# Layer 2's transform over d by frequency modulo four, a third X buffer, copies on another queue, and new orders in a two-layer spectral and mixer kernel

## The chip, the cores and the metric

The kernel runs on one core of a Trainium2 chip. Its time is the device time of one execution in microseconds (us), the median over runs. A core has a matrix engine, TensorE (PE in the profile, its weight loads PEld), a vector engine (DVE), a scalar engine (ACT), GpSimd (POOL), and SyncE (SP), whose queue here holds only DMA issues. Each engine works through its own instructions in the order in which the program wrote them; a semaphore holds an instruction until what it needs is there, and everything behind it on that engine waits with it.

## The reference

x has 2048 rows of 512 numbers. Two layers of the same form follow each other, each of two parts:

```python
x = x + _A_ref(_layernorm(x, axis=-1), A_w_r, A_w_i)
x = x + _B_ref(_layernorm(x, axis=-1), B_w1, B_w2, B_w3, B_w4)
```

`_A_ref` is a spectral filter: a real two-dimensional Fourier transform over rows and columns, a product with the complex table W = w_r + i w_i, and the transform back. `_B_ref` is a mixer: a layer norm, a product with w1 (512 x 512), a gelu, four column groups shifted by -1, +1, -2 and +2 rows, a product with w2 and a residual; then a layer norm, w3 (512 x 1792), a gelu, w4 (1792 x 512) and a residual.

## The kernel before, in words

Row s of x is row p of tile q with s = 16 p + q, so `K.x` holds 16 tiles q of 128 x 512. A layer's spectral part runs in these stages, and the letters are those of the order strings:

- front: per tile q the statistics of its rows (`s`, aggregated by `i`), the root (`S`), its reciprocal (`J`), the table T scaled by it (`Q`), then the transform over p as matmuls with x as the stationary operand (`O`), and copies out of PSUM into V (`G`). `over_p_quarters` issues eight matmuls a tile (four of 256 columns, four of 128), `over_p` four of 256, `over_p_plain` four of 128 whose sums and differences DVE forms while it copies (`fold_V`).
- d: the transform over d (`over_d`), copied to TV (`t`); q: the transform over q with the tables TL, in matmuls of 64 rows, two at a time (`over_q`), copied to X (`x`); p: the product with W on DVE (`weigh`), into PB; b: back over q with TR (`back_q`), copied to M (`m`). The unit is a block b of two frequencies over p, or a pair of blocks.
- D: back over d with G (`back_d`), copied to Y (`Y`); P: back over p (`back_p`), added to x by DVE (`a`).

The mixer follows: squares on ACT (`s`), statistics on POOL (`r`), root and reciprocal (`e`, `i`), the normed rows (`n`), transposed by DMA (`T`), w1 and its gelu (`v`, `h`), w2 (`u`), residuals (`f`, `E`), norm, transpose, w3 and gelu (`R`, `o`, `U`, `w`, `g`), w4 and the residual (`W`, `A`). The next layer's front is woven into the w3 and w4 work, and in the last layer the stores (`y`).

Three strings hold the order of all this, written out by hand or by a planner: `ORDER_0` for the first front, `ORDER_A` and `ORDER_B` for the two layers. An entry is a letter, a number (tile, block or pair) and, after it, the engine (A, V, P) or the PSUM bank (.0 to .7). `X` issues matmuls on zeros that only keep PE busy. In `first_front` the statistics of tiles 5 and 9 are made on ACT (`ON_ACT`), by two passes of ACT and, on POOL, `from_means` (L376 to L378, entry `f`). Entry `f2` also calls `load_tables` (L196, L188, L189), the POOL-issued loads of FL, TL and TR; `f3` stands behind it on POOL.

Layer 1's d works by the frequency modulo four (tables FL). Layer 2's d works with FA, by the frequency modulo two; W's columns are therefore permuted in place by DVE during layer 1's mixer (`permute`, entries `L`, L813 and L814), and G is loaded again in permuted order (`load_G2`). W comes in 16 loads on SyncE's queue; every second partition is a copy of its neighbour, made by four DMAs within SBUF (`double`), issued by POOL. All G, Tinv and MLP weights stand on SyncE's queue behind a small load that waits for the last of these copies.

## Time and profile before

| what | us |
|---|---|
| median of three runs | 347.29 (347.23 to 347.61) |
| profiled execution, first to last instruction (the span) | 345.6 |
| PE / DVE / ACT / POOL busy | 336.6 / 187.5 / 195.5 / 62.8 |
| w3 and w4 matmuls (L735, L755), together, on the chain | 56% of the span |
| first front matmul | 8.19 |
| last W load landed | 22.7 |

A table of stretches, used below, gives for a stretch of the span the busy time of each engine with its number of instructions, the granted clock of PE as a share, the DMA share and the rate in GB/s. A timeline line gives the start, the time from the first start to the last end, the engine and source line, the operation, out and in, and how many were merged; what ended idle time before them stands in brackets. A line of groups gives the busy time and mean ns of one, then the idle time ahead of it. An instruction's duration includes its latency, so the next one of the same kind starts before it ends.

The profile was taken in an execution of its own[...].

### The profile page before, as it was taken

The numbers are of one execution on the slowest core, as the hardware profiler recorded it, in microseconds if no ns is written. First come the engines' busy times: TensorE is split into PE (matmuls) and PEld (weight loads), VectorE is DVE, ScalarE is ACT, GpSimd is POOL, SyncE is SP. The second block draws the span as 40 slices with busy tenths as digits, with TensorE's granted clock in tenths as the row PEclk, the third lists the DMA queues.
The fourth block names the chain that finished last, engine by engine and source line by source line (L and its number), as shares of the span: only waits on it lengthen the run. The fifth ranks groups of instructions, "written<-read, shape, count | busy, mean of one in ns | idle before, by whom it ended". The sixth has DMA issues, their size and how long they took to land.

```text
span 345.6 us, 5672 instructions
## 1 busy us (share of the span) xinstructions
PE 336.6 (97%) x2161; PEld 190.3 (55%) x2178; DVE 187.5 (54%) x448; ACT 195.5 (57%) x348; POOL 62.8 (18%) x157
## 2 busy tenths in 40 slices
...
GB/s 259 280 361 236 383 173 101 84 62 0 3 61 21 33 24 14 49 13 1 2 0 2 2 2 44 99 97 41 27 2 61 0 108 0 46 14 95 0 32 76
DMA packets 45834, 25.12 MB, mean 73 GB/s; under 512 B 35008, under 2 KB 42816, under 8 KB 45808
## 3 DMA queue, kind: packets, MB, share of 16 engines
...
q10 hardware_dynamic: 240, 0.10, 0.1%
...
## 4 chain that ended last, share of the span: by engine, by line
PE 83%; ACT 7%; DVE 5%; DMA 3%; issue 2%; SPq 0%; ACTq 0%; DVEq 0%
PE ps L735 28%; PE ps L755 28%; PE ps L700 8%; PE ps L684 7%; PE ps L431 3%; PE ps L632 2%; PE ps L614 2%; ACT xn L306 2%; PE ps L644 1%; ACT hT L159 1%; DVE PB L603 1%; PE ps L584 1%; ACT X L159 1%; DVE X L157 1%; DVE x_state L652 1%
## 5 line engine op out<-in xcount | busy, mean ns | idle before, releaser
L742 ACT ACTIVATE gT<-ps 128x1024 bf16<-128x1024 f32 x56 | 56.6, 1023 | 80.4 <-PE ps L735 79.7
L735 PE MATMUL ps<-xT,w 128*128 128x512 bf16 x448 | 99.3, 379 | 0.0
L755 PE MATMUL ps<-w,gT 128*128 128x512 bf16 (+1 forms) x464 | 98.3, 366 | 0.6
L755 PEld LDWEIGHTS <-gT 128*128 128x128 bf16 x476 | 46.5, 98 | 50.1
L735 PEld LDWEIGHTS <-w 128*128 128x128 bf16 x448 | 43.8, 98 | 52.6
L761 DVE TENSOR_TENSOR x_state<-ps,x_state 128x512 bf16<-128x512 f32 (+1 forms) x34 | 22.1, 657 | 86.1 <-PE ps L755 78.9
L708 DVE SCALAR_TENSOR_TENSOR xn<-xn,ln_c,ps 128x512 bf16<-128x512 bf16 x32 | 23.5, 745 | 26.3 <-PE ps L700 19.5
L700 PE MATMUL ps<-w,hT 128*128 128x512 bf16 x123 | 28.8, 379 | 0.3
L684 PE MATMUL ps<-xT,w 128*128 128x512 bf16 x128 | 28.8, 379 | 0.2 <-DMA xT<-xn 0.2
L306 ACT ACTIVATE junk<-xn 128x512 bf16<-128x512 bf16 x32 | 19.9, 622 | 12.7 <-DVE xn L708 12.7
L652 DVE SCALAR_TENSOR_TENSOR x_state<-ps,x_state 128x512 bf16<-128x512 f32 x32 | 20.5, 686 | 4.2 <-PE ps L644 4.1
L294 DVE BATCH_NORM_STATS2 ln_st<-x_state 128x6 f32<-128x512 bf16 (+1 forms) x31 | 20.1, 663 | 3.7 <-DMA x_state<-in_A_x_dram 3.5
L700 PEld LDWEIGHTS <-hT 128*128 128x128 bf16 x128 | 12.4, 98 | 15.3 <-ACT hT L691 0.8
L684 PEld LDWEIGHTS <-w 128*128 128x128 bf16 x128 | 12.3, 98 | 15.3 <-DMA xT<-xn 1.4
L312 POOL TENSOR_SCALAR ln_mv<-ln_s 128x4 f32<-128x4 f32 x16 | 5.7, 357 | 80.3 <-DVE x_state L652 68.7
L306 ACT ACTIVATE xn<-x_state 128x512 bf16<-128x512 bf16 x32 | 20.0, 631 | 0.4 <-DVE x_state L652 0.2
L603 DVE TENSOR_TENSOR PB<-X,W 128x2048 bf16<-128x2048 bf16 (+1 forms) x20 | 19.4, 1010 | 0.2
L691 ACT ACTIVATE hT<-ps 128x512 bf16<-128x512 f32 x32 | 17.4, 604 | 2.5 <-PE ps L684 2.4
L314 POOL TENSOR_TENSOR ln_mv<-ln_s,ln_t 128x4 f32<-128x4 f32 x16 | 3.8, 239 | 80.1 <-ACT junk L306 73.5
L614 PE MATMUL ps<-TR,PB 128*128 128x128 bf16 x256 | 16.3, 219 | 0.1
L159 ACT ACTIVATE TV<-ps 128x1024 bf16<-128x1024 f32 (+1 forms) x16 | 14.2, 914 | 3.8 <-PE ps L560 2.3
L644 PE MATMUL ps<-Y,Tinv 128*128 128x256 bf16 x128 | 15.4, 272 | 0.5 <-ACT Y L159 0.2
...
## 6 DMA issues: line engine op xcount, KB each, us to landing
w<-in_B_w_dram SPq DMA_DIRECT2D x2, 1792.0 KB, 13.0
...
```

The lines of the kernel that those rows point to most:

```text
L159: K.nc.scalar.activation(dst, src, ACT.Copy, bias=0.0, scale=1.0)
L306: K.nc.scalar.activation(out, src, ACT.Square, bias=0.0, scale=D ** -0.5, accum_out=self.s[:, i, 1:2])
L603: nc.vector.tensor_tensor(t, X.pop(u)[:, 0:2 * n].unsqueeze(1).to_broadcast([P, 2, 2 * n, 256]), K.W[:, :, 2 * u:2 * u + 2 * n, 1:257], op ...
L614: nc.tensor.matmul(oh, lhsT=pab[u][:, k, 2 * (b - u) + h, F * P:(F + 1) * P], rhs=K.TR[:, k:k + 2, 2 * b + h], start=(k == 0), stop=(k == 1))
L652: nc.vector.scalar_tensor_tensor(K.x[:, q, :], ps.pop(("P", q)), 1.0, K.x[:, q, :], op0=ALU.mult, op1=ALU.add, accum_out=ln[g].s[:, i, 0:1])
L684: nc.tensor.matmul(o[:, i], lhsT=K.w1[:, t, j * P:(j + 1) * P], rhs=xT[g][:, :, t, :], start=(t == 0), stop=(t == 3))
L700: nc.tensor.matmul(o, lhsT=K.hT[:, j, st:st + P], rhs=K.w2[:, j, :], start=(j == 0), stop=(j == 3))
L708: nc.vector.scalar_tensor_tensor(xn[:, q, :], xn[:, q, :], ln[q // 4].c[:, q % 4:q % 4 + 1], ps.pop(("u", n)), op0=ALU.mult, op1=ALU.add, ...
L735: nc.tensor.matmul(o[:, i], lhsT=K.w3[:, c, t * P:(t + 1) * P], rhs=xT3[g][:, :, c, :], start=(c == 0), stop=(c == 3))
L742: nc.scalar.activation(gT[g][:, 2 * j:2 * j + 2, :], ps.pop(("w", k)), ACT.Gelu_apprx_tanh, bias=0.0, scale=1.0)
L755: nc.tensor.matmul(o, lhsT=gT[g][:, t, i * P:(i + 1) * P], rhs=K.w4[:, t, d], start=(t == 0), stop=(t == 13))
L761: nc.vector.tensor_tensor(x, ps.pop(("W", n)), x, op=ALU.add)
```

## The change

- Layer 2's d uses the same code and tables as layer 1's; FA, G2 and both permutations go. V is then needed in four quarters: `fold_V` makes two of them and the sums, `fold_again` (entry `I`, on DVE or POOL) the other two.
- Layer 2's front has six plain pairs where it had five; the others use `over_p_quarters`. That function interleaves the two tiles of a pair in PSUM, in runs of four columns, and the copies can be split in halves by block (`SPLIT_FIRST`, `SPLIT_V`, entries `L`).
- The four last blocks of back q are made and copied in halves (`SPLIT_B`, entries `V` and `l`), and back d is issued in two halves (`D` and `C`).
- X has three buffers, T's scaled tables eight where they had twelve.
- W's copies 1 to 3 are issued on SyncE's queue behind the W loads; copy 0 stays on POOL.
- POOL can take rows of a layer norm (`apply`), residuals (`resid`) and folds; ACT can make scaled tables in layer 2's front.
- All three orders are new. `FOLD`, `half_D` and `fold_D`, also new, are used by no entry.

Of `ORDER_A` and `ORDER_B` the diff below has the part up to the first w1 product. Of the code, some hunks are left out.

```diff
-    double = lambda k: q.dma_start(K.W[1::2, :, 8 * k:8 * k + 8], K.W[0::2, :, 8 * k:8 * k + 8])
+    double = lambda k, q=nc.gpsimd: q.dma_start(K.W[1::2, :, 8 * k:8 * k + 8], K.W[0::2, :, 8 * k:8 * k + 8])
 
     def load_tables():
-        spare = K.grp.tile([P, 4, 4, P], BF16, name="xT", bufs=4)
-        K.FL = spare[:, 0:2].rearrange("p a b c -> p (a b c)")[:, 0:768]
-        K.dummy = spare[:, 2, 0:1]
-        q.dma_start(K.FL, dram["FL"])
+        K.FL = K.const.tile([P, 768], BF16, name="FL")
+        q.dma_start(K.FL[:], dram["FL"])
         load_TL(0)
         load_TL(1)
         load_TR(0)
@@ -203,19 +196,12 @@
         gate = K.const.tile([1, 2], BF16, name="gate")
         q.tensor_copy(gate[:], after[0:1, 0, 0:2])
         turn_TL(K, slice(0, 8))
-        double(1)
         q.dma_start(K.TL[:, 1, 8:16], dram["TL2"])
-        double(2)
-        double(3)
         load_TR(1)
+        for k in range(1, 4):
+            double(k, nc.sync)
 
...
             setattr(K, k, t)
-        K.FA = K.const.tile(list(tabs["FA"].shape), BF16, name="FA")
-        for t in range(2):
-            nc.sync.dma_start(K.FA[:, t], dram["FA"][:, t])
 
...
-        if eng == "V":
-            self.K.nc.vector.tensor_scalar(dst, src, self.mv[:, i, 0:1], r, op0=ALU.add, op1=ALU.mult)
+        if eng in "VP":
+            e = self.K.nc.vector if eng == "V" else self.K.nc.gpsimd
+            e.tensor_scalar(dst, src, self.mv[:, i, 0:1], r, op0=ALU.add, op1=ALU.mult)
...
-    K.Tq[q] = K.stream.tile([P, 2, P], BF16, name="Tq", bufs=12)
+    K.Tq[q] = K.stream.tile([P, 2, P], BF16, name="Tq", bufs=8)
...
-def over_p(K, qs, split=False):
-
...
+def over_p_quarters(K, qs):
+
+    n = len(qs)
+    ps = banks(K, n)
     for i, q in enumerate(qs):
         T = K.Tq.pop(q)
-        plus, both, swap = T[:, 0], T[:], T[:, ::-1]
-        twice = lambda k: T[:, k:k + 1].to_broadcast([P, 2, P])
+        plus, both, swap = [v.rearrange("d k (b c) -> d k b c", c=4) for v in (T[:], T[:], T[:, ::-1])]
+        plus = plus[:, 0]
+        twice = lambda k: T[:, k:k + 1].to_broadcast([P, 2, P]).rearrange("d k (b c) -> d k b c", c=4)
         for h in range(2):
-            o = (ps[:, h, 0:256] if split else ps[:, i, h * 256:(h + 1) * 256]).rearrange("d (k p) -> d k p", k=2)
+            o = (ps[:, h] if n == 2 else ps[:, 0, h * 256:(h + 1) * 256]).rearrange("d (k b q c) -> d k b q c", k=2, q=n, c=4)
+            o = o[:, :, :, i]
             terms = ((0, o, twice(0)), (1, o[:, 1], plus), (3, o[:, 1], plus), (2, o, swap)) if h == 0 else \
                     ((1, o, swap), (0, o[:, 0], plus), (2, o[:, 0], plus), (3, o, twice(1)))
-            for n, (c, dst, rhs) in enumerate(terms):
-                K.nc.tensor.matmul(dst, lhsT=K.x[:, q, c * P:(c + 1) * P], rhs=rhs, start=(n == 0), stop=(n == 3))
...
-def fold_V(K, qs, ps, right):
+def fold_V(K, qs, ps, right, pairs):
+
     n, lo = len(qs), qs[0]
-    v = K.V[:].rearrange("d (t h) b q c -> d h t q b c", h=2)[:, :, :, lo:lo + n]
-    left = ps[:, :, 0:256].rearrange("d q (t b c) -> d t q b c", t=2, c=4)
-    right = right.rearrange("d q (t b c) -> d t q b c", t=2, c=4)
-    for h, op in ((0, ALU.add), (1, ALU.subtract)):
-        for t in range(2):
-            K.nc.vector.tensor_tensor(v[:, h, t], left[:, t], right[:, t], op=op)
-
-
-def take_V(K, qs, ps, eng, part=False):
+    row = lambda t: t.rearrange("d q (t b c) -> d t q b c", t=2, c=4)
+    v = K.V[:].rearrange("d t b q c -> d t q b c")[:, :, lo:lo + n]
+    for t in range(2):
+        K.nc.vector.tensor_tensor(v[:, 3 * t], row(ps[:, :, 0:256])[:, t], row(right)[:, t], op=ALU.subtract)
+    K.nc.vector.tensor_tensor(pairs, ps[:, :, 0:256], right, op=ALU.add)
...
+def fold_again(K, qs, pairs, eng):
+
+    n, lo = len(qs), qs[0]
+    e = K.nc.vector if eng == "V" else K.nc.gpsimd
+    row = pairs.rearrange("d q (t b c) -> d t q b c", t=2, c=4)
+    v = K.V[:].rearrange("d t b q c -> d t q b c")[:, :, lo:lo + n]
+    for t, op in ((1, ALU.add), (2, ALU.subtract)):
+        e.tensor_tensor(v[:, t], row[:, 0], row[:, 1], op=op)
...
+def take_V(K, qs, ps, eng, half=None):
 
     dst = K.V[:].rearrange("d t b q c -> d (t b) q c")[:, :, qs[0]:qs[-1] + 1:max(qs[-1] - qs[0], 1)]
-    if part:
-        t = "AV".index(eng)
-        dst, ps = dst[:, 64 * t:64 * t + 64], ps[:, t:t + 1, 0:256]
-    copy(K, dst, ps.rearrange("d q (tb c) -> d tb q c", c=4), eng)
+    src = ps.rearrange("d n (s q c) -> d (n s) q c", q=len(qs), c=4)
+    if half is not None:
+        lo = slice(16 * half, 16 * half + 16)
+        dst, src = [v.rearrange("d (t b) q c -> d t b (q c)", t=4)[:, :, lo] for v in (dst, src)]
+    copy(K, dst, src, eng)
...
-            if not last:
-                oi = o[:, i].rearrange("p (e r f) -> p e r f", e=2, r=4)
-                part = lambda k: V[:, k, 2 * b:2 * b + 2].rearrange("d b q c -> d (b q c)")
-                nc.tensor.matmul(oi[:, :, 3], lhsT=part(1), rhs=K.FL[:, 0:P].rearrange("p (e f) -> p e f", e=2),
-                                 start=True, stop=True)
-                nc.tensor.matmul(oi[:, :, 1], lhsT=part(2), rhs=K.FL[:, P:2 * P].rearrange("p (e f) -> p e f", e=2),
-                                 start=True, stop=True)
-                for k in range(2):
-                    rhs = K.FL[:, (k + 1) * 256:(k + 2) * 256].rearrange("p (e r f) -> p e r f", e=2, r=2)
-                    nc.tensor.matmul(oi[:, :, 0:3:2], lhsT=part(3 * k), rhs=rhs, start=(k == 0), stop=(k == 1))
-                continue
-            oi = o[:, i].rearrange("p (e h f) -> p h e f", e=2, h=2)
-            for h in range(2):
-                for t in range(2):
-                    nc.tensor.matmul(oi[:, 1 - h], rhs=K.FA[:, t, h],
-                                     lhsT=V[:, 2 * t + h, 2 * b:2 * b + 2].rearrange("d b q c -> d (b q c)"),
-                                     start=(t == 0), stop=(t == 1))
+            oi = o[:, i].rearrange("p (e r f) -> p e r f", e=2, r=4)
+            part = lambda k: V[:, k, 2 * b:2 * b + 2].rearrange("d b q c -> d (b q c)")
+            nc.tensor.matmul(oi[:, :, 3], lhsT=part(1), rhs=K.FL[:, 0:P].rearrange("p (e f) -> p e f", e=2),
+                             start=True, stop=True)
+            nc.tensor.matmul(oi[:, :, 1], lhsT=part(2), rhs=K.FL[:, P:2 * P].rearrange("p (e f) -> p e f", e=2),
+                             start=True, stop=True)
+            for k in range(2):
+                rhs = K.FL[:, (k + 1) * 256:(k + 2) * 256].rearrange("p (e r f) -> p e r f", e=2, r=2)
+                nc.tensor.matmul(oi[:, :, 0:3:2], lhsT=part(3 * k), rhs=rhs, start=(k == 0), stop=(k == 1))
...
-        X[u] = K.stream.tile([P, 4, 256], BF16, name="X", bufs=2)
+        X[u] = K.stream.tile([P, 4, 256], BF16, name="X", bufs=3)
...
-        both = TAKE_B[last][b] == "B"
-        ps["b", b] = o = banks(K, 1 + both)
-        for F in range(2):
+        ps["b", b, F] = o = banks(K, 1)[:, 0]
+        parts = (0, 1) if F is None else (F,)
+        for i, f in enumerate(parts):
             for h in range(2):
...
-    def back_d(m):
-        ps["D", m] = o = banks(K, 2)
-        for F in range(2):
-            for i in range(2):
-                for e in range(2):
-                    nc.tensor.matmul(o[:, i, e * 256:(e + 1) * 256], lhsT=M[:, F, e, 2 * m + i, :], rhs=K.G[:, F, e, :],
-                                     start=(F == 0 and e == 0), stop=(F == 1 and e == 1))
+        n = 512
+        if F is not None:
+            dst, n = dst[:, :, 2 * F:2 * F + 2], 256
+        copy(K, dst, ps.pop(("b", b, F))[:, 0:n].rearrange("f (h g q c) -> f h g q c", h=2, q=NQ, c=4), eng)
+
+    def first_half(b):
+        return 0 if b in SPLIT_B[last] else None
+
+    def back_d(m, F):
+        if F == 0:
+            ps["D", m] = banks(K, 2)
+        o = ps["D", m]
+        for i in range(2):
+            for e in range(2):
+                nc.tensor.matmul(o[:, i, e * 256:(e + 1) * 256], lhsT=M[:, F, e, 2 * m + i, :], rhs=K.G[:, F, e, :],
+                                 start=(F == 0 and e == 0), stop=(F == 1 and e == 1))
...
-    def resid(n):
-        nc.vector.tensor_tensor(K.x[:, ROWS[n], :], K.x[:, ROWS[n], :], xn[:, ROWS[n], :], op=ALU.add)
+    def resid(n, eng):
+        (nc.vector if eng == "V" else nc.gpsimd).tensor_tensor(K.x[:, ROWS[n], :], K.x[:, ROWS[n], :], xn[:, ROWS[n], :], op=ALU.add)
...
     def front(k):
         qs = [ROWS[n] for n in PAIRS[k]]
-        ps["O", k] = over_p_plain(K, qs) if k < PLAIN else over_p(K, qs, k >= 14)
-
-    def take_front(k, eng):
+        ps["O", k] = over_p_plain(K, qs) if k < PLAIN else over_p_quarters(K, qs)
+
+    def take_front(k, eng, half=0):
...
-                fold_V(K, qs, ps["O", k], ps["right", k][:])
+                ps["pairs", k] = K.stream.tile([P, 2, 256], FP32, name="pairs", tag="TV_Y", bufs=4)
+                fold_V(K, qs, ps["O", k], ps["right", k][:], ps["pairs", k][:])
...
-    def permute(k):
-
-        w = K.W[:, k // 8, 4 * (k % 8):4 * (k % 8) + 4, 1:257]
-        t = K.stream.tile([P, 4, 256], BF16, name="X", bufs=2)
-        tw = t[:]
-        nc.vector.tensor_copy(tw.rearrange("p b (h f) -> p b h f", h=2), w.rearrange("p b (f h) -> p b h f", h=2))
-        nc.vector.tensor_copy(w, tw)
...
-TAKE_B = ("FFFFFFFFFFFFFFFB", "FFFFFFFFFFFFFFFB")
+SPLIT_B = ((12, 13, 14, 15), (12, 13, 14, 15))
+SPLIT_FIRST = (5, 6, 7, 8)
+SPLIT_V = (6, 14, 15)
 ROWS = [*range(2, 16), 0, 1]
 PAIRS = {**{k: [2 * k, 2 * k + 1] for k in range(7)}, 14: [14], 15: [15]}
-PLAIN = 5
-FLEX = "mGnotxY"
+PLAIN = 6
+FLEX = "mlGLnotxYIKEpQ"
+FOLD = [(), ()]
...
 ORDER_0 = """
-s0 s1 s3 i1 i0 s2 s4 i3 i2 S0 J0 Q0V s5 i4 S1 J1 Q1A O0 s6 s7 i6 i7 s8 Q2A Q3A O1 f2 S2 J2 i8 Q6V Q7V s9 f3 s10 O3 Q4V
-Q5A s11 O2 G0A i10 i11 s13 S3 G1A J3 Q8V Q10A Q11A Q9V O4 s12 i13 i12 S4 G3A s15 s14 J4 i15 i14 Q12V S5 Q13V G2A G4A
-J5 Q14V O5 Q15V O6 G5V O7 G7A G6V O8 G8A G8V
+s0 s1 i0 i1 s2 s3 S0 J0 s5 i2 i3 Q1V Q0V O0.0 S1 J1 f2 s9 s8 s10 s11 i8 i10 f3 i11 s7 Q2A Q3A O1.2 S3 J3 Q11A i7 Q9A
+Q10A Q8V s6 s4 i6 i4 G1A s13 S2 J2 s12 Q4A O4.4 G4A Q6V Q5V i13 i12 s14 S4 Q7A J4 O5.6 s15 i14 i15 G0A Q12V Q13V S5
+G5A J5 O2.2 O3.4 L5A G3A Q14V Q15V G2V O6.0 L6V G6A O8.6 O7.7 G8A L8A L7A G7V
 """
...
 ORDER_A = """
-d0.3 t0V d1.6 d2.0 t1A q0.2 x0V p0 t2A q1.4 x1A p1 d4.6 t4A N0 d10.1 t10A q2.4 x2V p2 q4.6 d6.0 x4A t6A d12.3 t12A
-d14.5 q10.6 q6.0 d8.2 p4 x10A b4.4 x6V b3.7 d15.6 p10 t8A m4A t15A p6 q8.2 q12.0 b1.4 m3A x8A b0.6 b2.7 x12A b6.2 m2A
-t14V b5.3 m1V p8 q15.0 m0A q14.4 b10.7 x15A b9.6 p12 m6A m10V p15 b8.0 m5A x14A b7.2 m7A b11.3 m11A p14 b12.7 m8V
-b13.5 m9V b14.1 m12A b15.2 m13A m14A X4.0 m15A m15V D1.5 Y1A D0.0 Y0A D3.3 Y3A P2.5 a2 s2 P3.6 a3 s3 P0.0 a0 P7.2 s0
-P1.7 P6.5 D2.0 a1 s1 a7 s7 r0 a6 s6 Y2V e0 i0 n1V D5.6 Y5A n0V T0 D4.2 Y4A P4.0 a4 P5.4 a5 s4 n3V D7.5 s5 r1 Y7A n2V
-P8.7 P11.3 c0 a8 a11 e1 i1 n4V n5V T1 P10.4 D6.0 Y6A s8 a10 s10 P15.5 T2 P14.3 n7V n6V s11 P9.2 P12.0 c1 a9 s9 P13.4
...
+X4.0 d0.3 t0A d2.0 d1.5 q0.2 d4.6 t1A N0 t2V x0A p0V t4A q1.4 x1A q2.0 x2V d6.2 t6A d10.6 q4.4 p1V t10A d14.0 x4V t14A
+d8.2 q10.6 q6.4 t8A x10A p2V d15.0 x6A p4V b2.1 q14.2 x14A m2V d12.6 p10V q8.1 b1.5 t15A b3.0 t12A p6V x8A b10.4 q15.6
+m10A b0.3 x15A q12.1 p14V b4.4 b14.6 p8V m0A b11.7 m3V p15V b5.3 x12A b8.0 m11A b6.1 b15.2 p12V b7.7 m8V m4A b13.4 m1A
+m15A m5A m13V m6A b12.5 m12V m14A V15.2 b9.0 m9A V13.3 l13A V14.5 V12.4 m7V D0.6 D1.0 l14A l15V l12V C1 Y1A C0 D3.2 C3
+Y3A P2.0 P3.1 Y0V P1.7 D2.2 P0.6 a2 s2 C2 D5.4 C5 a3 s3 a1 s1 P7.7 D7.0 a0 s0 r0 Y2V Y5A a7 P5.6 P6.2 e0 i0 n1P n0P s7
+a5 s5 P4.3 a6 s6 a4 n3V s4 P11.4 D4.6 C4 C7 P10.5 D6.2 C6 T0 n2P Y7A T1 r1 Y4V P9.6 P8.7 e1 Y6A P15.0 P12.1 P13.2 a11
+i1 n6V s11 n7V T3 a9 s9 a10 s10 a8 s8 n5P P14.3 n4P v0.4 h0 r2 T2 v1.6 h1 a15 M1 a14 n11V n10V v3.4 T5 s15 n8P v2.6 M0
...
 """
 ORDER_B = """
-d15.7 t15V d4.1 t4V d1.3 t1A d8.6 q1.4 x1V t8A p1 q4.2 x4A q15.0 x15V p4 d12.4 t12A d10.6 q8.2 p15 q12.4 t10A b1.0
-d14.1 x12A t14A d2.6 m1A t2A x8V p8 d0.2 p12 b5.5 m5A t0A q10.0 x10V q2.3 x2A p10 d6.5 t6A b9.2 b4.1 b12.0 q14.6 q0.4
-m9A q6.2 m12A p2 m4A x0V b11.0 p0 x6A p6 b2.1 m2A b10.4 x14A b8.2 m8A m10A p14 b3.1 m3A b0.7 b7.5 m11A m0V b13.3 m13A
-b14.6 b6.2 m6A m7V m14V b15.4 m15A m15V D3.0 Y3A D2.4 Y2V D1.6 Y1A P6.0 a6 s6 D0.2 Y0A P4.4 a4 s4 P5.5 a5 P7.6 a7 s5
-P2.1 P1.4 a2 P0.2 a0 a1 s7 P3.6 r1 D5.0 a3 s2 s0 e1 i1 n5V n4V T2 D7.2 n6V n7V D4.4 T3 Y4V Y5A P11.1 P10.0 a10 s3 s1
-r0 Y7A e0 D6.6 i0 n2V P8.2 P9.5 n3V T1 Y6A a11 s10 n0V P14.3 n1A P13.0 P15.7 P12.1 a9 s11 s9 a8 s8 T0 a14 s14 a15 a13
...
+X4.4 d15.4 t15A d1.0 t1A d4.5 q15.1 x15V p15V d8.3 d12.0 t4A t12V q4.6 t8A d2.2 x4A q1.4 x1A d0.0 q12.6 t0A d10.4 q0.0
+t2V q2.2 t10A p4V q10.4 x0V p1V p0V b4.0 x2A p2V x10A q8.1 p10V d6.3 x8A b2.5 b15.1 x12A b0.2 b5.6 m2V m15V b11.7 t6A
+m0A d14.5 p8V q6.1 m11A b3.4 b1.7 t14A b9.3 x6A p12V b13.5 q14.1 m4A m1A b8.0 b12.7 m5V b10.6 p6V m3A b7.4 m13V x14A
+b6.1 m8A p14V b14.0 m7V m9A V14.2 m10A m6V V13.3 V15.4 m12A m14A l15A V12.5 D2.6 l12A l13V l14A D3.0 C3 C2 D1.3 C1 Y3A
+P7.2 Y1A Y2V a7 s7 P6.0 D0.6 P4.1 a6 C0 a4 P5.3 a5 P2.0 P3.1 s6 Y0A s4 D4.2 P1.5 s5 P0.4 D5.6 C5 a2 a3 C4 s3 r1 e1 a1
+D6.0 C6 a0 i1 n7V s1 s2 D7.4 Y4V n4V n6P C7 n5V s0 P8.2 P9.3 Y5A P10.6 a8 P11.7 r0 e0 i0 T3 n0V T2 M0 n1P Y6A P13.2
+n3P P12.0 Y7A P14.1 n2V a11 s8 s11 a10 s10 T0 P15.7 a9 s9 a12 a15 v2.5 a14 r2 n9V n8P h2 s12 n10V v3.3 n11P s14 T1
```

## The prediction

> **What bounds the kernel now.** I read the chain of work that ended last first, then the busy time by stretches of the span, then the timelines of PE and POOL inside the stretches where PE is not simply streaming.
>
> ```profile
> PE 83%; ACT 7%; DVE 5%; DMA 3%; issue 2%; SPq 0%; ACTq 0%; DVEq 0%
> ```
>
> PE sets the end. I cut the span where the stages change: before the first front matmul, front of layer 1, d/q/weigh/back-q of layer 1, back-d/back-p of layer 1, MLP of layer 1 with most of layer 2's front, rest of that front, then the same stages of layer 2.
>
> ```profile
> core 0: us, PE busy (x) PEld busy (x) DVE busy (x) ACT busy (x) POOL busy (x), PEclk, DMA share, GB/s
> 8.19:19.48 11.29, 10.88 (x128) 9.73 (x128) 11.15 (x36) 10.10 (x22) 6.54 (x13) 1.00 0.98 307
> 19.48:38.05 18.57, 18.43 (x260) 15.15 (x260) 17.02 (x22) 17.38 (x27) 3.38 (x6) 1.00 0.90 307
> 38.05:52.46 14.41, 14.22 (x129) 12.52 (x130) 10.82 (x33) 13.23 (x29) 4.30 (x15) 1.00 0.81 236
> 52.46:178.73 126.27, 125.85 (x617) 59.31 (x623) 72.44 (x186) 61.84 (x108) 24.63 (x54) 1.00 0.18 32
> 178.73:182.96 4.23, 4.15 (x42) 3.38 (x39) 3.97 (x13) 3.38 (x6) 0.00 (x0) 1.00 0.00 0
> 182.96:202.79 19.83, 19.15 (x257) 16.37 (x258) 18.74 (x23) 17.04 (x26) 0.00 (x0) 1.00 0.01 2
> 202.79:217.44 14.65, 14.36 (x129) 12.50 (x130) 11.75 (x32) 12.64 (x29) 2.25 (x10) 1.00 0.20 38
> ```
>
> In 52.46:178.73 DVE and ACT are half idle: only PE work counts there. In the two d/q/back-q stretches all three engines are near full, so less PE work alone cannot buy its whole price. In 8.19:19.48 PE streams from the first row to the last.
>
> ```profile
> 182.96 2.79 PE L560 MATMUL ps<-FA,V 128*128 128x256 bf16 x24
> 185.68 1.05 PE L584 MATMUL ps<-TV,TL 64*128 64x256 bf16 x16
> 186.86 1.91 PE L560 MATMUL ps<-FA,V 128*128 128x256 bf16 x16
> 188.70 1.05 PE L584 MATMUL ps<-TV,TL 64*128 64x256 bf16 x16
> 189.68 0.62 PE L614 MATMUL ps<-TR,PB 128*128 128x128 bf16 x8
> ```
>
> Taking one 0.27 us latency off, a 256-column matmul is issued every 0.109 us (2.52 over 23) and, from the 16 L441 matmuls that take 0.89 in the chain, a 128-column one every 0.056. A pair of 64-row matmuls takes 0.106. The second L560 run ends its issue at 186.86 + 16 x 0.109 = 188.60, and L584 starts at 188.70: 0.10 lost; eight pairs later, 189.55, L614 starts at 189.68: 0.13 lost, 0.2 to 0.25 a q run.
>
> ```profile
> 8.43 0.23 POOL L378 TENSOR_SCALAR ln_mv<-ln_mv 128x1 f32<-128x1 f32 x1
> 8.71 0.82 POOL L196 DMA_DIRECT2D xT<-tab_FL  x1
> 9.54 1.07 POOL L188 DMA_DIRECT2D TL<-tab_TL  x2
> 10.60 0.74 POOL L189 DMA_DIRECT2D TR<-tab_TR  x1
> 11.36 0.21 POOL L376 TENSOR_TENSOR ln_mv<-ln_s 128x1 f32<-128x1 f32 x1
> 11.92 0.21 POOL L378 TENSOR_SCALAR ln_mv<-ln_mv 128x1 f32<-128x1 f32 x1
> ```
>
> The variance of row 9 (f3, the last two lines) cannot start before POOL has issued the four table loads.
>
> [...] The trace has only these relatives:
>
> ```profile
> L254 POOL TENSOR_SCALAR TL<-TL 128x512 bf16<-128x512 bf16 x1 | 1.7, 1669 | 0.1
> L255 POOL COPY TL<-TL 128x512 bf16<-128x512 bf16 x1 | 0.7, 746 | 0.0
> ```
>
> [...] The new front writes runs of four with gaps of four; no run here shows such a write, and I take no cost.
>
> **The change part by part**, against the profiled execution (span 345.6; median of the runs 347.29, so 1.7 lie around the span, which I leave alone).
>
> PE work. Layer 2's d goes from 64 x 0.109 = 6.98 to 32 x 0.109 + 32 x 0.056 = 5.28: -1.70. Layer 2's front: 40 x 0.056 + 24 x 0.109 = 4.86 becomes 48 x 0.056 + 16 x 0.109 + 16 x 0.056 = 5.33: +0.47. The order cuts q into 8 runs per layer where PE had 5 and 4: 7 x 0.2 = +1.4. Fills 11 to 8, all in idle time: 0. The PE sum hardly moves (+0.2); the time goes where waits go.
>
> Front of layer 1. DVE has one statistic less ahead of the first scaled table: PE starts near 7.84, not 8.19. But ACT now makes row 9's sums (1.23) before tables 2 and 3, so these come at 9.4 and 9.8, and PE ends O1 at 10.8 (idle 0.3). The next front is rows 8 to 11, not 6, 7, 4, 5. Its root S3 waits for f3; POOL ends f2 at about 8.15, the loads at 10.85, f3 at 11.6. Root 0.3, reciprocal 0.15, one scaled table 0.3, waits between: O4 at 12.55. Idle 1.75. DVE stands at that reciprocal meanwhile, and behind it queue the statistics of rows 6, 4, 13, 12, so nothing else can fill PE. From there 12 rows x (4 x 0.109 + 4 x 0.056 = 0.66) = 7.9, and 0.25 for row 4's table: last matmul at 20.7, before 18.47. The last copy is now split by b, 0.35 and about 0.4 of latencies: first d at 21.45, before 19.48: **+2.0**. From below 0 if the root is not late; above 2.4.
>
> d/q/back-q, both layers. I followed the three orders by hand with start-to-start times from the timelines (ACT 0.91, 0.48, 0.29 for 1024, 512, 256 elements; DVE 1.13, 0.60, 0.34; weigh 1.14 and 0.61). Layer 1: copies sum to 17.0 on ACT and 16.8 on DVE, first copy 0.57 after d starts; x8 at 11.0, p12 at 14.6 and the last first-half copy at 18.2, so D0 at 18.3 against 18.57: **-0.3** (-0.9 to +0.8). Layer 2: ACT 17.2, DVE 16.2; PE waits at d12 for x15, at q10 for t10 (0.6), at q8 for x2, at b5 for x12; last first-half copy 18.8, D2 at 18.9 against 19.83: **-0.95** (-1.9 to 0). The third X buffer helps here: x0, x2 and x10 no longer wait for the product two before. Back d in halves: same matmuls, D of two pairs covers the last four copies.
>
> W copies on SyncE: nothing. They stand behind the last W load (landed 22.7); each moves 514 KB, so I expect 24 to 27 us, and p4, p10, p14 come at about 29, 31, 33. If late, each microsecond is paid. TL's turn waits on POOL for the last scaled table (18.6 here) and ends at 21.1; q0 needs it at 22.8. The gate and the MLP weights behind them were at 28.5, so they don't slip; the FA loads in front of the first transposes (landed 47.9) go.
>
> Back d/back p of layer 1. The rows 1, 0, 2 are normalised on POOL in a row, then 5 and 4; DVE took 0.33 each. From D0: row 0 is added at 5.8, its squares end at 6.6, POOL 7.2, root 7.7, reciprocal 7.9, so three norms take 8.0 to 8.0 + 3c, and the second transpose lands 3.2 later: v0 at 11.3 + 3c. PE is ready at 14.3. c lies between 0.75 (the copy[...]) and 1.67 (the tensor-scalar row, whose elements are strided): I take 1.2, v0 at 14.9 against 14.41: **+0.5**. Ends: -0.3 at 0.75; at 1.67 v0 is at 16.3 and rows 5 and 4, behind on POOL, hold v3 by another 1.3: +3.2. Layer 2 has one POOL norm at this place: **-0.2**.
>
> MLP of layer 1: PE only. One more plain pair (8 x 0.056) stands ahead of the last half of W14: **+0.45**. From that to d the chain (add, statistic, root, table, front, copies) is 4.1 against 4.23: 0. W is no longer permuted: 17.9 of DVE go, under PE; nothing now, and no cover lost. POOL's residuals, folds and norms have 126 us to hide in. MLP of layer 2 and the tail: 0 (-0.3 to +0.5).
>
> Sum: 2.0 - 0.3 - 0.95 + 0.5 - 0.2 + 0.45 = +1.5: **348.8**.
>
> **Rivals.** (a) Faster: the three X buffers and halved copies let the copying engines run without gaps. The last copies would then end at 0.6 + 17.0 and 0.6 + 17.2, not 18.7 and 19.6 as walked: 1.1 and 1.9 less, 345.8. For it: ACT is busy 17.0 of 19.83 now. Against: copies alternate with matmuls on eight banks, and q is cut finer. It passes the kernel before when half of its 3.0 comes. (b) POOL norms at 1.67: 351.5; for it the only tensor-scalar row, against it its stride. (c) The root S3 isn't late, because the loads issue faster or in another place: 346.8, no measurable change. Against: the trace shows that queue in order. (d) The strided front output doubles the issue time of the 128 matmuls of layer 1: +10, 358.
>
> **How the numbers follow.** Forecast 40%, (a) 20%, (b) 20%, (c) 13%, (d) 3%, a mixture of smaller stalls above the forecast 4%. 0.2% (0.7 us) is about what a measurement can tell. Faster takes (a) almost whole and part of (c): 0.23; the same, the rest of (c) and the low edge of the forecast: 0.16; slower 0.61. The range runs from (a) to (b): 345.7 to 351.8; the forecast's own is 347.8 to 349.8.
>
> **What would show it.** PE idle before the front of rows 8 to 11, with S3's root released by POOL, and first d near 21.4; 18.3 and 18.9 from first d to first back d; POOL's norm rows near 1.2 us and w1's first matmul released by the transpose DMA; the MLP stretches of unchanged length but 0.45. I am wrong if S3 is released by DVE before 11, or if a W copy or a stride in PSUM shows up on the chain.

## The result and the profile after

The changed kernel takes 350.11 us (median, 349.86 to 351.22) against 347.49 for the kernel before on the same chip: a ratio of 1.0065, 95% interval 1.0046 to 1.0084. It is slower by 2.6 us, where 1.5 were forecast (348.8). The profiled execution has a span of 348.5, 2.9 more than before's 345.6. The times of the changed kernel's ten runs lie 1.73 to 2.03 us above their spans, those of the kernel before, in the runs timed beside the experiments, 1.79 to 1.91. The ten runs of the kernel before on this chip fall in two groups, six near 347.3 and four near 348.8 (in later groups of runs, most of the slower ones show a mean granted clock of 0.994), so its median lies 0.2 above that of the six, and against these the difference is 2.85.

The chain of waits of the changed kernel, by engine, has the same share of PE as before; DMA has gained one hundredth and POOL two.

```profile
PE 83%; ACT 5%; DMA 4%; DVE 4%; POOL 2%; issue 1%; ACTq 0%; POOLq 0%; DVEq 0%
```

The same stretches as before, cut where the stages change in the changed kernel (columns as in the table of stretches above):

```profile
core 0: us, PE busy (x) PEld busy (x) DVE busy (x) ACT busy (x) POOL busy (x), PEclk, DMA share, GB/s
7.89:22.57 14.68, 11.80 (x133) 10.12 (x132) 11.22 (x36) 11.07 (x25) 7.78 (x15) 1.00 0.95 315
22.57:41.02 18.45, 18.23 (x257) 14.27 (x257) 16.82 (x21) 17.38 (x28) 0.24 (x1) 1.00 0.71 221
41.02:55.68 14.66, 14.36 (x129) 12.44 (x129) 12.81 (x33) 12.03 (x29) 5.69 (x13) 1.00 0.84 254
55.68:182.84 127.16, 126.77 (x631) 59.80 (x631) 57.10 (x142) 63.72 (x113) 40.94 (x78) 1.00 0.16 30
182.84:186.97 4.13, 3.85 (x47) 3.23 (x44) 3.38 (x10) 3.44 (x10) 0.00 (x0) 1.00 0.00 0
186.97:205.91 18.94, 18.47 (x256) 14.15 (x256) 16.38 (x21) 17.45 (x28) 0.00 (x0) 1.00 0.01 2
205.91:220.23 14.32, 14.27 (x128) 12.39 (x129) 11.85 (x33) 13.01 (x30) 4.70 (x12) 1.00 0.20 38
```

Only one row is out of scale: in the front of layer 1 PE is busy 11.80 of 14.68 us, where it was busy 10.88 of 11.29. Row by row against before:

| stage | before | after | measured | forecast |
|---|---|---|---|---|
| up to the first d (start and front of layer 1) | 19.48 | 22.57 | +3.09 | +2.0 |
| d/q/back-q, layer 1 | 18.57 | 18.45 | -0.12 | -0.3 |
| back d/back p, layer 1 | 14.41 | 14.66 | +0.25 | +0.5 |
| MLP of layer 1 with most of the next front | 126.27 | 127.16 | +0.89 | +0.45 |
| rest of that front | 4.23 | 4.13 | -0.10 | 0 |
| d/q/back-q, layer 2 | 19.83 | 18.94 | -0.89 | -0.95 |
| back d/back p, layer 2 | 14.65 | 14.32 | -0.33 | -0.2 |
| MLP of layer 2 and the tail | 128.16 | 128.27 | +0.11 | 0 |
| sum | 345.6 | 348.5 | +2.9 | +1.5 |

So layer 2's d/q/back-q is 0.9 shorter, as forecast, though d, the order and the third X buffer changed there together, and the front of layer 1 takes it back three times over. The timeline of the changed kernel in the middle of that front:

```profile
8.32 0.82 POOL L189 DMA_DIRECT2D FL<-tab_FL  x1
9.15 1.08 POOL L183 DMA_DIRECT2D TL<-tab_TL  x2
10.21 0.74 POOL L184 DMA_DIRECT2D TR<-tab_TR  x1
...
11.54 0.22 POOL L360 TENSOR_SCALAR ln_mv<-ln_mv 128x1 f32<-128x1 f32 x1
...
11.80 0.30 ACT L364 ACTIVATE ln_r<-ln_mv,eps 128x4 f32<-128x4 f32 x1 [1.94 <-POOL ln_mv L360]
...
12.68 0.49 PE L403 MATMUL ps<-Tq,x_state 128*128 128x256 bf16 x4 [1.69 <-DMA W<-in_A_w_r_dram]
```

ACT's root (S3) waits 1.94 us for POOL, whose last step of row 9's variance stands behind four DMA issues; PE starts rows 8 to 11 at 12.68. The releaser that the profile names for PE, a DMA of W, is the last to come of several semaphores on paper only: the chain goes POOL, ACT's root, the scaled table. And at the end of the front:

```profile
20.63 1.43 ACT L154 ACTIVATE V<-ps 128x512 bf16<-128x512 f32 x4 [0.67 <-DVE V L152]
...
22.09 0.42 DVE L152 CAST V<-ps 128x256 bf16<-128x256 f32 x1 [1.49 <-ACT V L154]
...
22.57 0.23 PE L545 MATMUL ps<-FL,V 128*128 128x128 bf16 x1 [0.69 <-DVE V L152]
```

The last front matmul ends at 20.98 and the first d starts at 22.57. Between them ACT waits for a copy of DVE, and then DVE for all four of ACT's.

### The profile page after: what moved, and what is told of

It is laid out like the page before. It is cut to its first block, busy times and chain, and to the rows that moved or that the text cites. A ratio compares the mean times of both kernels' runs of the same rounds, so it can differ in the third digit from the quotient of the medians.

```text
span 348.5 us, 5716 instructions
## 1 busy us (share of the span) xinstructions
PE 337.9 (97%) x2191; PEld 187.6 (54%) x2191; DVE 166.8 (48%) x382; ACT 195.3 (56%) x358; POOL 95.7 (27%) x196
## 4 chain that ended last, share of the span: by engine, by line
PE 83%; ACT 5%; DMA 4%; DVE 4%; POOL 2%; issue 1%; ACTq 0%; POOLq 0%; DVEq 0%
PE ps L752 28%; PE ps L732 28%; PE ps L697 7%; PE ps L681 7%; PE ps L593 4%; DMA xT<-xn 3%; PE ps L613 2%; PE ps L569 2%; ACT xn L289 2%; PE ps L551 2%; DMA x_state<-in_A_x_dram 1%; ACT Y L154 1%; PE ps L403 1%; PE ps L641 1%; DVE PB L582 1%
## 5 line engine op out<-in xcount | busy, mean ns | idle before, releaser
L739 ACT ACTIVATE gT<-ps 128x1024 bf16<-128x1024 f32 x56 | 55.8, 1023 | 91.9 <-PE ps L732 89.8
L752 PE MATMUL ps<-w,gT 128*128 128x512 bf16 (+1 forms) x476 | 99.4, 367 | 0.0
L295 POOL TENSOR_SCALAR ln_mv<-ln_s 128x4 f32<-128x4 f32 x16 | 4.4, 274 | 65.3 <-DVE x_state L649 63.9
L403 PE MATMUL ps<-Tq,x_state 128*128 128x256 bf16 (+1 forms) x160 | 14.2, 246 | 3.5 <-DMA W<-in_A_w_r_dram 1.7
L613 PE MATMUL ps<-G,hT 128*128 128x256 bf16 x128 | 15.8, 273 | 0.0
```

The lines of the kernel that those rows point to most:

```text
L613: nc.tensor.matmul(o[:, i, e * 256:(e + 1) * 256], lhsT=M[:, F, e, 2 * m + i, :], rhs=K.G[:, F, e, :], start=(F == 0 and e == 0), stop=(F ...
L739: nc.scalar.activation(gT[g][:, 2 * j:2 * j + 2, :], ps.pop(("w", k)), ACT.Gelu_apprx_tanh, bias=0.0, scale=1.0)
L752: nc.tensor.matmul(o, lhsT=gT[g][:, t, i * P:(i + 1) * P], rhs=K.w4[:, t, d], start=(t == 0), stop=(t == 13))
```

## The experiments

Unless a line says otherwise, the edits start from the changed kernel. Each group of runs had runs of the kernel before on its chip (medians 347.56, 347.44, 347.31 and 347.28), and ratios are to those. The stages of all runs, from their profiles (us):

| kernel | median | ratio, 95% interval | first front matmul to first d | d/q/back-q 1 | back d/p 1 | v0 to first d of layer 2 | d/q/back-q 2 |
|---|---|---|---|---|---|---|---|
| before | 347.49 | | 11.29 | 18.57 | 14.40 | 130.5 | 19.83 |
| after | 350.11 | 1.0065 (1.0046 to 1.0084) | 14.67 | 18.45 | 14.66 | 131.29 | 18.95 |
| e1_means_first | 348.9 | 1.0032 (1.0021 to 1.0044) | 13.52 | 18.46 | 14.33 | 131.69 | 18.95 |
| e2_last_copies | 349.45 | 1.0046 (1.003 to 1.0061) | 13.78 | 18.44 | 14.31 | 131.83 | 18.95 |
| e3_front_before | 347.99 | 1.0009 (0.9992 to 1.0025) | 11.71 | 18.46 | 14.31 | 131.85 | 18.96 |
| e4_copies_pool | 349.94 | 1.0057 (1.0037 to 1.0077) | 14.89 | 18.46 | 14.32 | 131.74 | 18.95 |
| e5_both | 348.41 | 1.0019 (1.0003 to 1.0036) | 12.84 | 18.75 | 14.33 | 131.91 | 18.96 |
| e6_transposes | 350.23 | 1.0084 (1.0069 to 1.0099) | 14.69 | 18.46 | 14.33 | 131.9 | 18.96 |
| e7_x_two | 354.08 | 1.0205 (1.0182 to 1.0229) | 14.71 | 21.84 | 14.33 | 131.65 | 20.81 |
| e8_norms_dve | 350.95 | 1.0105 (1.009 to 1.012) | 14.69 | 18.46 | 15.06 | 131.64 | 18.96 |
| e9_mixer_dve | 349.53 | 1.0055 (1.0037 to 1.0074) | 14.69 | 18.46 | 14.31 | 131.09 | 18.97 |
| e10_both_pool | 347.88 | 1.0013 (0.9998 to 1.0028) | 12.43 | 18.91 | 14.32 | 131.67 | 18.95 |
| e11_all | 346.8 | 0.9981 (0.9967 to 0.9995) | 11.49 | 18.72 | 14.32 | 131.08 | 18.95 |
| e12_tr_first | 347.96 | 1.0004 (0.9986 to 1.0022) | 12.68 | 18.45 | 14.68 | 130.73 | 18.95 |

The two d/q/back-q stages come back within about 0.02 us where no edit touches them (look down the last column), so there a stage tells more than the median. Others move more. The first front matmul waits for loads of x and lay between 7.33 and 8.34. The start of v0 depends on the issue time of one transpose (1.4 to 1.8 us behind the one before it). From v0 to layer 2's first d the kernels with the mixer of the changed kernel took 131.64 to 131.91, where the changed kernel itself, with a late v0, has 131.29.

### The loads behind the variance: e1

```diff
-TABLES = 2
+TABLES = 3
```

> The changed kernel with the table loads called at f3, behind the statistics of row 9, in place of at f2 (TABLES = 3). Theory (the root S3 is late because row 9's three POOL steps stand behind four DMA issues): ACT's sums end at 9.07, so f3 ends near 9.95 and S3 starts near 10.0 (11.80 in the changed kernel); DVE still makes row 7's statistics ahead of the reciprocal, which starts near 10.6; rows 8 to 11 start near 11.15 in place of 12.68, first d near 21.05 in place of 22.57, and the kernel is 1.5 us shorter, about 348.6. Rival one (DVE's statistics bound this front, the idle time comes back further on): first d no earlier than 22.2, gain below 0.4. Rival two (the loads, now 1.6 us later on POOL, become late): the first q run or the negation of TR waits for a table load, and the gain is lost there.

Measured: 348.9, 1.2 less; first d at 21.38 in place of 22.57. The timeline of this kernel (ACT's root, and the run of front matmuls):

```profile
10.09 9.71 PE L403 MATMUL ps<-Tq,x_state 128*128 128x256 bf16 x112 [0.74 <-ACT Tq L385]
...
10.54 0.30 ACT L364 ACTIVATE ln_r<-ln_mv,eps 128x4 f32<-128x4 f32 x1
```

The root is no longer late: PE runs 112 front matmuls in one stretch from 10.09, and rows 8 to 11 wait for nothing. The root is at 10.54 and not at 10.0 because in this execution the tile of x with row 9 came later (ACT waited 0.53 us for it and began its sums at 8.30, not 7.73); that is also why first d moved by 1.2 here and not by 1.5. The medians differ by 1.2 as well; whether the tile was late in those runs too is not shown. Both rivals fall: the statistics are not the bound, and no load is late (the next stage is 18.46).

### The halves of the last copies: e2

```diff
-... G2V O6.0 L6V G6A O8.6 O7.7 G8A L8A L7A G7V
+... G2V O6.0 G6A L6A O8.6 O7.7 G8A L8A G7V L7V
```

> The changed kernel with the last copies of layer 1's front dealt out differently: both halves of pair 6 and of tile 15 on ACT, both halves of tile 14 on DVE, so that no two halves of one tile are copied by two engines. In the changed kernel ACT sat idle 0.67 us until DVE had copied a half of pair 6, and DVE 1.49 us until ACT had copied a half of tile 14; the last front run ends at 20.98 and first d starts at 22.57. Theory (the two halves of a tile wait for each other across engines): first d at 21.5 to 21.7, about 1.0 us earlier, and the kernel about 349.1 to 349.4. Rival (the copying engines, not the order of the halves, set the first d): first d moves by less than 0.3, or moves and the first d/q/back-q stage grows by as much, and the time stays at 350.1 within 0.4.

Measured: 349.45, and 13.78 from first front matmul to first d, 0.9 less. In this kernel's timeline DVE's two halves of tile 14 wait for PE alone:

```profile
20.59 0.76 DVE L152 CAST V<-ps 128x256 bf16<-128x256 f32 x2 [1.09 <-PE ps L403]
...
21.16 0.22 PE L545 MATMUL ps<-FL,V 128*128 128x128 bf16 x1
```

The first d follows the first of those halves. So the two halves of a tile had been made to wait for each other, across engines, over V or over the PSUM bank that both read. Two things in the traces speak for the bank. In the changed kernel ACT and DVE write other tiles into V at the same time (ACT from 18.93 to 19.96, DVE from 18.78 to 20.00). And in the timeline of the kernel before, two engines copy the two halves of tile 15 side by side:

```profile
19.00 0.38 ACT L159 ACTIVATE V<-ps 128x256 bf16<-128x256 f32 x1
19.25 0.42 DVE L157 CAST V<-ps 128x256 bf16<-128x256 f32 x1
```

There each half lies in a bank of its own, while the new halves, cut by block, both come out of the same bank or banks. No run changes the bank alone, so that it is the bank is not shown.

### Both, and where the next bound lies: e5, e4, e10

e5 has both edits above.

> Both edits of the front together: the table loads behind row 9's statistics, and the halves of the last copies dealt out so that no tile is shared by two engines. Theory (two separate delays, one in the middle of the front and one at its end): the gains add, 1.2 and 0.65 us by the medians of the two single runs, so 348.2, and first front matmul to first d about 12.6 us (14.67 in the changed kernel, 13.52 and 13.78 in the single runs). Rival (both edits move the same bound, the work of DVE and ACT in the front): no more than the larger gain, 348.9, and that stage at 13.4.

Measured: 348.41 (expected 348.2); the stage is 12.84. Most of what it still has over the 11.29 of before lies in one wait, seen in this kernel's timeline:

```profile
8.04 0.63 ACT L352 ACTIVATE junk<-x_state 128x512 bf16<-128x512 bf16 x1 [0.73 <-DMA x_state<-in_A_x_dram]
...
9.28 0.89 ACT L385 ACTIVATE Tq<-T,ln_r 128x256 bf16<-128x256 bf16 x2
```

ACT makes the sums of row 9, whose tile of x came late, ahead of the tables of rows 2 and 3, and PE waits 0.95 us for these tables until 9.82; another 0.34 is in the step from the last front matmul to first d (0.68, where before had 0.34). The front's gains add, but 0.30 comes back in d/q/back-q of layer 1, 18.75 in place of 18.45. DVE's timeline in that stage:

```profile
30.47 4.11 DVE L582 TENSOR_TENSOR PB<-X,W 128x2048 bf16<-128x2048 bf16 x4 [0.79 <-ACT X L154]
```

ACT's copy to X had ended at 29.62; DVE's wait before this product (p10) ended at 30.43, and the copy of W that it needs, issued on SyncE's queue, landed at 30.39. With the slow front the same copies had been hidden:

```diff
         turn_TL(K, slice(0, 8))
+        double(1)
         q.dma_start(K.TL[:, 1, 8:16], dram["TL2"])
+        double(2)
+        double(3)
         load_TR(1)
-        for k in range(1, 4):
-            double(k, nc.sync)
```

> The changed kernel with W's copies 1 to 3 on POOL's queue, issued where they were before. In the changed kernel the third copy landed at 32.28 (28.49 before) and the last MLP weight at 51.32 (47.21 before). Theory (no one waits for either): no difference, 350.1 within 0.4, and first d to first back d 18.45 within 0.2. Rival (the copies on SyncE's queue hold up the products with W or, through the small load behind them, the first transposes): 0.4 us or more shorter.

Measured: 349.94, the stage 18.46: no difference. The same edit on top of e5 (its expectation calls the waiting product p4; it is p10):

> The kernel of e5_both with W's copies 1 to 3 on POOL, where they were before. With the changed front the copies were hidden (e4_copies_pool: the same time). In e5_both the first d starts at 20.24, the second copy on SyncE's queue landed at 30.39, and DVE's product p4 waited for that semaphore until 30.43, with DVE idle 0.79 us. Theory (the copies on SyncE's queue are the next bound as soon as the front is shorter): p4 starts near 29.7, first d to first back d 18.45 in place of 18.75, and 0.3 us less than 348.41. Rival (the copies land no earlier on POOL, or POOL's issues hold up the rest of its work): 348.4 or more.

Measured: 347.88, 0.5 less than e5, but the stage did not go to 18.45: it is 18.91. The timeline of this kernel:

```profile
29.37 4.10 DVE L583 TENSOR_TENSOR PB<-X,W 128x2048 bf16<-128x2048 bf16 x4
...
31.82 0.61 PE L594 MATMUL ps<-TR,PB 128*128 128x128 bf16 x8 [0.30 <-DMA TR<-tab_TR]
```

The product comes 1.1 us earlier (0.23 of it by an earlier first d) and with no wait. Now PE waits for the last load of TR, which stood behind the copies on POOL's queue and landed at 31.78 (28.60 in e5). What is gained over e5 lies in the front (12.43 against 12.84): PE's wait for the tables of rows 2 and 3 is 0.56 there, not 0.95, because row 9's tile came earlier (ACT's sums start at 7.83, not 8.04). I do not count it for the copies. The last of these transfers lands at about the same time either way (32.28, a copy of W, in the changed kernel; 32.63, TR, in e4): the choice of queue and of order decided who is last.

### The transposes of the mixers: e6 and e9

In the changed kernel PE waits for T7, by its timeline:

```profile
73.52 1.67 PE L681 MATMUL ps<-xT,w 128*128 128x512 bf16 x7 [0.39 <-DMA xT<-xn]
```

The expectations count such a wait from start to start of the matmuls, which gives 0.56 here.

```diff
-... n15V n12V k2 f0 E0V E3P n13A h5 v4.1 u4.0 h4 u6.6 n14V T6 u5.5
+... n15V n14V n12V k2 f0 E0V n13A h5 v4.1 u4.0 h4 u6.6 T6 E3P u5.5
```

and in layer 2 `T0` and `T1` moved up behind `n3P` and `n2V`.

> The changed kernel with two places of the orders mended where PE waited for a transposed tile in the mixers. Layer 1: row 14 is normed right behind row 15, and the residual that POOL makes (entry E3) stands behind the issue of T6, so that T6 and T7 are issued about 0.9 us earlier (68.86 and 70.27 in the changed kernel; PE then waits 0.56 us at 73.52 for T7). Layer 2: T0 and T1 stand right behind the norms that fill them, where they stood behind nine further entries of the order (T1 was issued at 220.94 though its rows were ready at 219.91; PE waits 0.71 us at 224.40). Theory (only these transposes were late): both waits go, 1.2 us less, 348.9. Rival (the engines that make the rows, or the 1.3 us for which SyncE issues one transpose, are the bound and the wait comes back at the next transpose): less than 0.4.

Measured: 350.23, nothing gained. In layer 1 T6 is issued at 69.00, T7 at 70.29, and PE waits 0.63 near 73.57, more than the 0.39 of the changed kernel. In layer 2 the wait for T1 did fall, from 0.55 to 0.22. The timeline of this kernel:

```profile
66.91 2.02 DVE L373 TENSOR_SCALAR xn<-x_state,ln_mv,ln_r 128x512 bf16<-128x512 bf16 x3
66.99 1.15 POOL L712 TENSOR_TENSOR x_state<-x_state,xn 128x512 bf16<-128x512 bf16 x1
```

The edit of E3 was empty: the transpose is on SyncE, so POOL, which works through its own instructions, made the residual at about the same moment as before (66.99, where the changed kernel had 67.17), and DVE's first norm beside it took 1.38 us, the other two 0.40. Taking the work off POOL:

```diff
-... n15V n12V k2 f0 E0V E3P n13A h5 v4.1 u4.0 h4 u6.6 n14V T6 u5.5
+... n12V n15V n14V k2 f0 E0V n13A h5 v4.1 u4.0 h4 u6.6 T6 E3V u5.5
-... n1P Y6A P13.2 n3P P12.0 Y7A P14.1 n2V ...
+... n1P Y6A P13.2 n3V T0 P12.0 Y7A P14.1 n2V T1 ...
```

> The changed kernel, in the two places of e6_transposes again, with the work taken off POOL as well: layer 1's residual E3 on DVE, behind the norms of rows 12, 15 and 14, and layer 2's norm of row 3 on DVE. In e6_transposes POOL's residual ran beside DVE's three norms, which took 1.38, 0.40 and 0.40 us, and T6 was issued at 69.00. Theory (a norm on DVE waits while POOL works, and that made the transposes late): the norms take 0.41 each, T6 is issued at 67.9 and T7 at 69.3, PE's wait of 0.56 to 0.79 us near 73.5 goes; in layer 2 T1 is issued 0.5 us earlier and the wait of 0.71 near 224.4 falls below 0.2; together 1.0 us less, 349.1. Rival (DVE's extra work delays the additions to x in turn, or something else holds the transposes): less than 0.4 gained, 349.7 to 350.3.

Measured: 349.53, 0.6 less (1.0 expected). DVE's timeline in the same place:

```profile
66.94 1.05 DVE L373 TENSOR_SCALAR xn<-x_state,ln_mv,ln_r 128x512 bf16<-128x512 bf16 x3
```

And PE's, where the wait for T7 was:

```profile
72.81 2.54 PE L681 MATMUL ps<-xT,w 128*128 128x512 bf16 x11
```

Three norms in 1.05 us, T6 at 67.93, T7 at 69.26, and PE goes on without a wait: the theory holds for layer 1. In layer 2 the wait for T1, counted from start to start, fell from 0.71 to 0.22 (it was 0.38 in e6), but T1 still went out 1.69 us behind T0, not at once, and back d/back p there became 14.47 (14.32), so DVE's extra norm cost 0.15. What holds T1 is open. In e6 it was issued at 221.00, just after POOL's first statistics step of the next group (220.67 and 0.24 long), though its rows were ready at 219.98; but in e9 it went out at 220.17, ahead of that step (220.51), so the step is not what it waits for.

### The norms of layer 1 back on DVE: e8

```diff
-... e0 i0 n1P n0P s7 ... T0 n2P Y7A T1 ...
+... e0 i0 n1V n0V s7 ... T0 n2V Y7A T1 ...
```

> The changed kernel with the rows 1, 0 and 2 of layer 1's norm on DVE in place of POOL. In the changed kernel POOL took 0.76 us a row, T0 was issued at 50.67, T1 1.83 later behind T0's issue, and v0 started at 55.68, 0.44 us after PE could have. Theory of the prediction's step (the norms on POOL set v0): T0 issued 0.8 us earlier, v0 at PE's readiness, first back d to v0 14.3 in place of 14.66, and the kernel 0.3 to 0.4 us shorter, 349.7 to 349.8. Rival (PE itself is the bound there by now, and three norms more on DVE hold up the additions to x that free PE's banks): no gain or up to 0.3 longer.

Measured: 350.95, 0.8 longer; first back d to v0 is 15.06. The timeline of the changed kernel at this place:

```profile
49.12 2.27 POOL L373 TENSOR_SCALAR xn<-x_state,ln_mv,ln_r 128x512 bf16<-128x512 bf16 x3 [0.79 <-PE ps L641]
...
55.68 1.67 PE L681 MATMUL ps<-xT,w 128*128 128x512 bf16 x7 [0.19 <-DMA xT<-xn]
```

And the timeline of e8, where two of the norms are DVE's:

```profile
48.52 0.73 DVE L373 TENSOR_SCALAR xn<-x_state,ln_mv,ln_r 128x512 bf16<-128x512 bf16 x2
...
49.92 1.47 PE L613 MATMUL ps<-G,hT 128*128 128x256 bf16 x12 [0.48 <-DVE x_state L649]
...
52.92 2.78 PE L641 MATMUL ps<-Y,Tinv 128*128 128x256 bf16 x24 [0.22 <-DVE Y L152]
55.54 1.67 PE L681 MATMUL ps<-xT,w 128*128 128x512 bf16 x7
```

T0 did go out 0.8 us earlier, counted from the first back d (8.80 against 9.65), but the two norms stood ahead of an addition to x that frees a bank, and PE waited 0.48 for it and later 0.22 for DVE's copy to Y. T1 was not late: it landed at 54.81, and v0 at 55.54 waits for nothing but PE. So the rival holds: PE's work and DVE's additions are the bound here, and with this order POOL is the right place for these norms. The loss was larger than the rival's 0.3.

### Two X buffers: e7

```diff
-        X[u] = K.stream.tile([P, 4, 256], BF16, name="X", bufs=3)
+        X[u] = K.stream.tile([P, 4, 256], BF16, name="X", bufs=2)
```

> The changed kernel with two X buffers in place of three. What the prediction said of the third one: in layer 2's d/q/back-q stage three copies to X no longer wait for the product two before. Theory (a good part of the 0.89 us that this stage gained comes from that buffer): layer 2's stage goes from 18.95 to 19.3 or more, layer 1's from 18.45 to 18.6, and the kernel is 0.4 to 0.8 us longer, 350.5 to 350.9. Rival (PE's shorter d and the order made the whole gain): both stages within 0.1, the time at 350.1 within 0.3.

Measured: 354.08, 4 us longer, where the theory had 0.4 to 0.8. Layer 2's stage goes from 18.95 to 20.81 and layer 1's from 18.45 to 21.84. PE's longest wait in layer 1, from the timeline of e7:

```profile
34.30 0.92 PE L569 MATMUL ps<-TV,TL 64*128 64x256 bf16 x7 [1.42 <-ACT X L154]
```

Two stretches around it, from e7's table of stretches (the last but two of the columns is the granted clock):

```profile
31.02:34.43 3.41, 1.82 (x24) 1.11 (x21) 3.41 (x4) 2.58 (x4) 0.00 (x0) 1.00 0.39 110
34.43:37.84 3.41, 3.41 (x33) 2.78 (x29) 2.11 (x4) 2.15 (x3) 0.00 (x0) 0.50 0.93 288
```

ACT, which copies to X, waits for DVE's product (0.67 and 0.69 us at 30.78 and 33.66), PE waits for ACT, and after that wait PE's granted clock is 0.50 for 3.41 us. So layer 1's loss of 3.39 is partly clock in this execution, which took 355.70; the three others, at a mean clock of 1.00, took 353.89 to 354.09, so I estimate the clock's part at 1.6 and the buffer's at 1.8. Layer 2's 1.86, at a clock of 1.00, is the buffer alone. These orders were written for three buffers: the run tells what the orders need, not what a third buffer would have brought the orders before.

### The front as before, and two versions that join the parts: e3, e11, e12

e3 has `ORDER_0` as it was before, with `G8A` in place of `G8A G8V` and `SPLIT_FIRST = ()`.

> The changed kernel with the order string of layer 1's front as it was before (no halves; tile 15 in one copy on ACT, where before two engines took a half each). It tells how much of the difference is the front of layer 1. Theory (the front costs 3.1 us: first d at 22.57 against 19.48, and everything else together 0.2 less): first d near 19.6, the kernel at 347.0 to 347.4, the same as the kernel before within 0.2%. Rival (the later stages only looked better because they started later, W and TL being there already): the d/q/back-q stage of layer 1 grows from 18.45 by 0.5 us or more, with a wait for a copy of W in it, and the kernel stays above 348.

Measured: 347.99, the kernel before within 0.2%, and 18.46 in the next stage: the rival falls. By the medians this front is worth 2.1 of the 2.6 us that the change lost, by first d 2.5. It is 0.6 above what was expected; 0.4 of that is seen between front and first d (11.71, where before had 11.29), tile 15 now being one copy on ACT, not two on two engines; the rest is not explained.

e11 takes e3, the mixer edits of e9, the copies of e10, and both halves of tile 15 on ACT:

```diff
-SPLIT_FIRST = (5, 6, 7, 8)
+SPLIT_FIRST = (8,)
-... G8A L8A L7A G7V
+... J5 Q14V O5 Q15V O6 G5V O7 G7A G6V O8 G8A L8A
```

> What the runs so far point to, put together: the changed kernel with layer 1's front in the order of before (e3_front_before; tile 15 now in two halves, both on ACT), the mixer edits of e9_mixer_dve, and W's copies on POOL. Theory (the parts add: front -2.1 by the medians of e3_front_before, the halves -0.25, the mixer -1.0): 346.7, which is 0.2% shorter than the kernel before. Rival (the mixer edits bring nothing, as in e6_transposes): 347.7, the kernel before within 0.2%.

Measured: 346.8, a ratio of 0.9981 (0.9967 to 0.9995): 0.5 us shorter than before and 3.3 us shorter than the changed kernel. In e11 the d/q/back-q stage of layer 1 is 18.72, with the wait for TR seen in e10. e12 moves that one load:

```diff
         double(2)
-        double(3)
         load_TR(1)
+        double(3)
```

> The kernel of e11_all with one line moved: the last load of TR stands on POOL's queue between the second and the third of W's copies, not behind the third. In e10_both_pool PE waited for that load (landed 31.78, the next back-q run at 31.82, 0.30 us idle by the profile), which took back what the earlier copies had given; in e11_all it landed at 31.14 and PE's next back-q run started 0.27 us late at 31.18. Theory (one queue, each transfer some 2 to 3 us behind the one before): TR lands near 29, the third copy near 31, just ahead of the product that needs it (31.2), and first d to first back d is 18.45 in place of 18.72: 0.25 us less, 346.5. Rival (the third copy is now late in its turn): no gain, 346.8 or more, and DVE waits for the copy near 31.2.

Measured: TR landed at 29.76, the third copy at 31.79, nothing waited for either, and the stage is 18.45, as expected. But the median is 347.96. In five of the fourteen executions, the profiled one among them, PE's mean clock was 0.995 and not near 1.0; in the profiled one it was 0.50 from 7.84 to 11.26 us, and the front took 12.68 in place of 11.49. Five more took 348.0 to 348.8 at a mean clock of 1.00, and of these no trace was kept. The shortest executions of the two are level (346.27 and 346.34). So the stage's gain is shown, a gain of the kernel over e11 is not, and whether the moved load has a part in the slower executions stays open. Nor would I build on e11's 0.5 us: its interval leaves out 1, but the same kernel with one load moved had a median 1.2 us longer.

## Why the prediction was right or wrong

**Direction and mechanism: right.** Slower, because the root of rows 8 to 11 stands behind POOL's table loads. Its times hold to 0.3 us up to the end of the front's matmuls: PE starts at 7.89 (7.84), row 9's variance ends at 11.76 (11.6), rows 8 to 11 start at 12.68 (12.55), the last front matmul ends at 20.98 (20.7). e1 shows the cause by removing it. Rival (c), that the root isn't late, falls with it; the 348.9 of e1 is what it would have given, not the 346.8 put down for it, since the other delay stays.

**The term that was too small: the step "the last copy is now split by b, 0.35 and about 0.4 of latencies".** It took 1.6 from the last matmul to the first d, where the step has 0.75. The step counted one half copy; it did not see that the new halves of a tile on two engines come one after the other, where the halves of before overlapped, and that DVE's half stood behind ACT's four. That is 0.9 of the 1.1 missing here (e2). It is also the main reason that 350.11 lies just above the forecast's own range (347.8 to 349.8).

**MLP of layer 1: +0.45 forecast, +0.89 measured.** Taken up to the first d of layer 2, that is +0.79 in the changed kernel, where v0 was late, and +1.1 to +1.4 in the others with this mixer. The plain pair is there; besides it PE waits for T7 near 73.5. The step "POOL's residuals, folds and norms have 126 us to hide in" is what failed: a residual on POOL held up DVE's norm beside it. e6 and e9 tell it apart from the order of the transposes; with it mended the stretch is 131.09, 0.59 above before. POOL's work on whole rows did so in e6: one norm took 1.38 us beside POOL's residual of 1.15, and 0.40 once that had ended. POOL's steps on 128x4 elements did not: in e9 one ran for 1.02 us from 67.54, and the norm that DVE began at 67.59 took 0.40. By what means a norm is held up, no run shows. The step priced POOL's own time and not what it costs DVE.

**d/q/back-q: -0.95 forecast, -0.89 measured in layer 2; -0.3 and -0.12 in layer 1.** The walk through the orders held, down to the 0.6 us that PE waits at q10 for t10:

```profile
194.76 0.61 PE L569 MATMUL ps<-TV,TL 64*128 64x256 bf16 x8 [0.35 <-ACT TV L154]
```

This timeline line of the changed kernel stands 0.57 us later than the run before it would have let it start. So d's 1.70 us less on PE is worth about half, as said, and rival (a), copies without gaps, is wrong. PE's busy time in this stage fell by 0.68 (19.15 to 18.47), so about three quarters of the gain is PE's own work, in which d's 1.70 and the finer q runs (+0.2 each in the prediction) pull opposite ways; what the copying engines set of the rest, no run tells apart. To the third X buffer the prediction gave no figure of its own; without it these orders lose 1.9 in layer 2, more than the whole gain.

**Back d/back p of layer 1: +0.5 forecast, +0.25 measured, and about -0.1 in most other runs (14.31 to 14.33).** The step's c is 0.76 (2.27 for three), the low end, not 1.2; rival (b) at 1.67 is wrong, and e8 shows that POOL helps here. The tensor-scalar row at 1.67 (L254, POOL on 128x512 in the trace of before) did not tell it; its elements are strided, and whether that is the reason no run tells. Left out of the step was that SyncE issues the second transpose only 1.4 to 1.8 us after the first, which hid the cheaper norms.

**W copies on SyncE at nothing: right for this kernel (e4), for a reason that was too narrow.** The landings were put at 24 to 27, the MLP weights "don't slip"; two copies landed at 24.13 and 26.16, but the third at 32.28 and the last weight at 51.32 (47.21 before). Neither was waited for. The step's own "if late, each microsecond is paid" came true as soon as the front was shorter (e5).

**Rival (d), the strided PSUM output: wrong.** The front matmuls of the changed kernel are issued 0.109 and 0.055 us apart (256 and 128 columns), as before. The doubling was the author's supposition, with no run behind it; these runs of four do not show it.

**POOL's time for the table loads: it held.** The four issues took 2.65 us before and 2.63 in the changed kernel, and the forecast rests on that time alone. In the trace of before SyncE's issues of W took 0.58 to 0.96 us each, about as long as one of POOL's.
